# Weight loads in two halves, a limit on the bytes in flight, and a new order of the first 840 pieces of a pooled-attention and gated-MLP kernel

## The chip, the cores and the metric

The kernel runs on one core of a Trainium2 chip. The metric is the device time of one execution in microseconds (us). Engines are named as the profile names them: PE is TensorE (matmuls), PEld its weight loads, DVE is VectorE, ACT is ScalarE, POOL is GpSimd, and SP is the queue that issues the DMA transfers.

## The reference

For each of 8 batches and 8 heads (576 positions, 64 wide) two attentions are added: one over queries, keys and values averaged in groups of 4 (144 positions), repeated 4 times, and a banded one in which position i sees the positions less than 4 away. The heads joined give x, 576 x 512 per batch. An MLP with a spatial gate follows.

```python
def _attn_ref(q, k, v):
    q_d = q.reshape(B, H, Sd, factor, D).mean(axis=3)
    out_up = np.repeat(sm_attn(q_d, k_d, v_d), factor, axis=2)
    mask = np.abs(pos[:, None] - pos[None, :]) < factor
    scores = np.where(mask, scale * np.matmul(q, k.transpose(0, 1, 3, 2)), -1000000000.0)
    ...
    return (out_up + np.matmul(attn, v)).astype(np.float32)

def _moe_ref(x, w_in, g_ln, w_sg, b_sg, w_out):
    h = x @ w_in
    h = 0.5 * h * (1.0 + np.tanh(c * (h + 0.044715 * h ** 3)))
    u, v = (h[..., :d_ff // 2], h[..., d_ff // 2:])
    v_n = (v - mu) / np.sqrt(var + 1e-06) * g_ln
    v_s = np.einsum('ts,bsd->btd', w_sg, v_n) + b_sg[None, :, None]
    return (x + (u * v_s) @ w_out).astype(np.float32)
```

`w_in` is 512 x 1024, `w_sg` 576 x 576, `w_out` 512 x 512.

## The kernel before

The work is cut into 2,109 named pieces. Each piece is a small function that emits the instructions of one step, and `ORDER` is a stored list of the names, in which they are emitted. A letter behind a slash says which engine does a piece that several could do (V is VectorE, A ScalarE, P GpSimd). All engines take their instructions in this order, so `ORDER` sets each engine's queue, the SP queue among them. `place` hands out the numbered buffers (8 of PSUM, 10 called X, 38 called R) along the same list.

The 64 heads are taken as 32 pairs g = 0 to 31, four per batch. The pieces of a pair: `lq`, `lk`, `lv`, `lw` load query, key, the values for the averaged attention and the values for the band; `qs`, `ks` sum groups of 4; `S` and `Y` are the band's and the averaged scores (`YS` both together from pair 4 on); `mx`/`my` take row maxima, `ia`/`ib` subtract them from the first pairs' scores, `ea`/`eb`/`es`/`ec` are exponentials and their sums, `re`/`rc` reciprocals, `np`/`nq` normalise; `T`, `t`, `U` transpose the probabilities on TensorE, `pa` to `pe` copy them to SBUF; `D` is the product with the values; `oe`, `od`, `xa`, `xb` merge the two attentions into x; `xh`, `xl`, `xc` split x in a high and a low part, since the dense matmuls run in a rounded format and are done three times (high x high, high x low, low x high).

The weights arrive as 64-bit words. `w_in`'s second half comes as `wy0` to `wy3`, its first half as `wz0` to `wz3`, `w_out` as `wr0` to `wr3`, each 512 KB; `wq0` to `wq4` are `w_sg`'s rows. For each of the first twelve, `w` loads it, `wu` scales the low word (ScalarE), `wq` scales the high word (VectorE or ScalarE), `wb` moves its bits (two VectorE instructions), `wt` adds (GpSimd), and `wh`, `wl` make the high and the low part. Of the MLP of batch b, `vk`, `v` are the gate's matmuls (of batch 0 one per pair, line 743), `u` those of the other half, `s` the spatial matmul, `o` the last one (line 821); the rest is activation, normalisation and stores.

Transfers are issued by `dma` on the SP queue. A transfer waits until the one issued six before it has landed (`DEPTH = 6`). `S0` and `S3` are preceded by 28 and 20 matmuls on zeros (line 976).

Of the kernel before, what the change touches and what calls it, by code (L numbers as in the profile page):

```python
# [94 lines left out]
wuy3 wqy3/A nq2/P U2 t2 xa0 xb0 ks5/P wby1 xh0/A YS4 pb2/A pc2/A nq3/P np3/P xl0/P t3 lw1 wuy1 wty1 pe2/A whz0/A
wlz0/P ma4 my4 ny4/A mb4 U3 wz2 wqz2/A lv2 ec4 T3 pa3/A pb3/V pc3/A pe3/A D1 mx4 wby3 wty3 lq5 qs5/V wbz2 nx4/A why1/A
wly1/P oe1/A od1 lw3 wuz2 YS5 ma5 vk3.0 xa1 xb1 vk1.0 lv3 ea4 mb5 vk0.0 wtz2 mx5 eb4 whz2/A re4/A my5 ny5/V lw2 nx5/A
D2 why3/A xh1/V ec5 vk2.0 wty2 xl1/V vk3.1 lv4 vs4 D3 wlz2/V rc4 nq4/P wr2 why2/A wly2/P oe2/V od2 xa2 xb2 wq0 wz1 lq6
eb5 ea5 xh2/A wq1 np4/V vk2.1 oe3/V od3 xa3 vk0.1 xb3 xh3/V xl3/P whq0/A U4 xl2/V wly3/V whq1/A wqz1/A t4 re5/A T4
pa4/A vk1.1 pb4/A pc4/A wur2 wbz1 wuz1 xc2 xc0 xc1 vk0.2 wtz1 wqr2/V wbr2 rc5 nq5/P lv5 lk6 np5/P ks6/V pe4/A vk2.2  # L100
v0.2 vg0.2 wq2 wq3 whq3/A wlq3/P vk1.2 v0.0 vg0.0 qs6/V vb0.2 v0.1 vg0.1 lw4 D4 YS6 whq2/A whz1/A wlz1/P my6 ny6/A lq8
ma6 mb6 ec6 mx6 nx6/A oe4/V wlq1/V lk7 vs5 wlq0/P vk3.2 od4 xa4 T5 vk4.0 eb6 vk4.1 ks7/V pa5/V vb0.0 vp0.0 lq7 qs7/V
vk4.2 ea6 re6/A u0.4 rc6 qs8/V u0.2 xb4 t5 u0.5 ua0.4 xc3 v0.4 ua0.5 ua0.2 U5 va0.4/A pb5/V pc5/A vb0.1 u0.3 nq6/P
np6/P lk8 v0.3 ks8/V pe5/A lw5 D5 lv6 ua0.3 vp0.2 vg0.3 vn0.0 vh0.0/A lw7 wr1 wr3 YS7 lw6 vp0.1 vn0.1 wq4 whq4/A b lq9
wlq2/V vj0.4 ma7 vl0.0/P mb7 vh0.1/A vs6 vl0.1/P T6 vg0.4 vn0.2 oe5/V pa6/A my7 ny7/V ec7 wlq4/P u0.7 vb0.3 vb0.4
vp0.3 od5 xa5 t6 u0.6 ua0.6 u0.1 ua0.7 vp0.4 U6 pb6/A mx7 pc6/A pe6/V vh0.2/A u0.0 xb5 xh5/A ua0.0 vn0.4 vn0.3 vh0.4/V
vh0.3/V vl0.3/P ua0.1 nx7/A ea7 eb7 re7/A vl0.2/V D6 YS8 lk10 vl0.4/V s0.0 s0.2 my8 wr0 wqr3/V ma8 oe6/V mb8 mx8 lv7
sa0.0 od6 vs7 lk9 sm0.0/V xa6 xb6 ny8/A s0.3 s0.1 rc7 lq10 ec8 xh4/A s0.4 wbr3 sa0.2 np7/V T7 pa7/A nq7/V ks9/V U7
ks10/V nx8/A qs10/V wur0 pb7/A pc7/A sa0.1 t7 pe7/A s0.5 wqr1/A wur3 sm0.2/P sa0.4 D7 xh6/A xl5/P wqr0/V qs9/V YS9 lv8
lk11 lq11 sm0.4/V eb8 sm0.1/P sa0.3 sm0.3/P xl6/P wbr1 s0.6 ma9 oe7/V od7 xa7 xb7 ea8 xl4/P re8/A s0.7 mb9 mx9 nx9/V  # L110
wur1 sa0.5 wtr3 xh7/A xl7/P v1.2 rc8 my9 sm0.5/V eb9 ny9/A ec9 np8/V T8 nq8/V u1.1 ea9 pa8/V t8 re9/A wbr0 gh0.2/A
sa0.7 wtr1 whr1/V whr3/A sa0.6 vg1.2 vb1.2 rc9 lw8 U8 pb8/A pc8/A pe8/A gh0.1/A np9/V v1.1 vg1.1 xc7 vs8 D8 oe8/A od8
xa8 lv9 YS10 ks11/V ma10 mb10 xb8 u1.4 qs11/V mx10 nx10/V u1.0 ua1.0 ua1.1 wtr0 v1.0 vp1.2 vs9 nq9/P wlr3/V my10 vb1.1
wlr1/P vp1.1 gl0.2/V xc6 whr0/V T9 ea10 pa9/A U9 pb9/V ny10/V xh8/V wlr0/V gl0.1/V gh0.0/A lk12 ec10 ks12/V pc9/V t9
pe9/V sm0.6/V u1.3 xl8/V u1.2 ua1.2 wtr2 xc5 whr2/A ua1.4 wlr2/V u1.5 xc4 u1.6 lq12 vn1.1 ua1.3 lw9 vg1.0 vb1.0 D9
ua1.5 YS11 ma11 mb11 eb10 re10/A sm0.7/P gl0.0/P my11 v1.3 v1.4 vp1.0 vn1.0 gh0.3/V gl0.3/V o0.2 vg1.3 rc10 np10/P T10
nq10/V oe9/V od9 xc8 lv10 vs10 ua1.6 lq13 va1.4/A o0.4 vh1.1/A vj1.4 vg1.4 ny11/A ec11 vb1.4 vp1.4 lw10 pa10/V xa9
o0.0 vn1.2 vn1.4 vh1.2/V xb9 o0.6 t10 qs12/P u1.7 oa0.2 vh1.0/A U10 mx11 vh1.4/A oa0.0 pb10/A vb1.3 pc10/V pe10/V
oa0.4 vl1.4/V oa0.6 vl1.2/P vp1.3 nx11/A eb11 o0.3 ea11 vn1.3 oa0.3 vl1.0/V o0.7 oa0.7 re11/A rc11 D10 YS12 my12
ny12/A lv11 oe10/V vl1.1/P vh1.3/A vl1.3/P qs13/V np11/P ma12 mb12 o0.1 oa0.1 lk14 lw11 od10 nq11/P mx12 s1.0 sa1.0  # L120
o0.5 xa10 T11 xb10 U11 pa11/V ec12 sm1.0/V ks14/P nx12/A eb12 s1.2 sa1.2 pb11/V ea12 re12/A rc12 xh10/A xl10/V s1.4
t11 oa0.5 pc11/A pe11/A nq12/V s1.1 sa1.1 sm1.2/V sa1.4 vs11 D11 oe11/A od11 lk13 os0.0 xh9/A ks13/P YS13 lk15 my13
np12/P ma13 mb13 xa11 xb11 ny13/A xl9/V s1.3 xh11/A t12 sm1.4/V U12 sm1.1/P sa1.3 s1.6 mx13 nx13/A T12 pa12/A pb12/V
pc12/A pe12/A s1.5 s1.7 xl11/P sm1.3/P gh1.1/A sa1.5 sm1.5/V lq14 ec13 os0.2 lv12 os0.3 v2.0 u2.6 ks15/P eb13 vs12
qs14/P sa1.6 ea13 re13/V ua2.6 rc13 ua1.7 vg2.0 v2.3 os0.1 np13/P T13 pa13/A gh1.0/V gl1.0/P lw12 sm1.6/V D12 lv13
oe12/A sa1.7 sm1.7/V gh1.3/V gl1.3/V gl1.1/V YS14 nq13/P U13 od12 xa12 gh1.2/A lw13 t13 vg2.3 vb2.0 xc11 ma14 mb14
gl1.2/P lq15 o1.4 my14 pb13/V xb12 ny14/V vs13 mx14 v2.1 ec14 lq16 o1.0 pc13/V nx14/A vp2.0 vn2.0 vh2.0/V pe13/V D13
oa1.4 ea14 qs15/V eb14 oa1.0 YS15 my15 re14/V ny15/V ec15 ma15 mb15 mx15 rc14 v2.2 vg2.2 lk16 xc10 xc9 v2.4 lv14 vg2.1
vs14 np14/V vb2.1 T14 lw14 va2.4/A vj2.4 nx15/A nq14/P vl2.0/V oe13/A od13 xa13 xb13 ks16/P vp2.1 qs16/V vn2.1 vh2.1/A
# [906 lines left out]
```

## Time and profile before

| what | us |
|---|---|
| median of 3 runs | 577.85 (575.29 to 580.2) |
| the profiled execution | 577.51 |
| span in it, first to last instruction | 575.7 |
| mean granted TensorE clock | 0.993 |

The profile cuts the span into stretches and says how long each engine was busy in each. A row of the order of time gives start, length, engine, line, operation, what is written and read, a count, and in brackets how long the engine idled before and what released it ("issue" is time for which the profile shows no releaser). The span is read against TensorE: what its matmuls take is fixed by the computation, so its idle time is what an order can change.

### The profile page before, as it was taken

How to read it: one execution, taken by the hardware profiler on the slowest of the kernel's cores; microseconds unless marked ns; L12 is line 12 of the kernel's file. 1: busy time of each engine (PE TensorE's matmuls, PEld its weight loads, DVE VectorE, ACT ScalarE, POOL GpSimd, SP SyncE). 2: the span in 40 equal slices, each digit the busy share in tenths (PEclk: the TensorE clock that was granted, in tenths of full speed). 3: DMA queues.
4: the chain of work that ended last, by engine and by line, in shares of the span. 5: the costliest groups of instructions: out<-in, count | busy, mean ns of one | idle time of the engine just before them, and what ended most of it. 6: DMA issues, size and time to landing. Idle time of an engine off the chain costs nothing.

```text
span 575.7 us, 17465 instructions
## 1 busy us (share of the span) xinstructions
PE 557.2 (97%) x7032; PEld 521.3 (91%) x7032; DVE 422.9 (73%) x944; ACT 343.9 (60%) x1165; POOL 314.7 (55%) x395
## 2 busy tenths in 40 slices
...
GB/s 291 281 251 332 164 148 84 41 60 77 121 158 173 23 109 55 210 59 2 87 56 201 134 44 99 53 139 98 104 66 196 105 106 2 17 23 41 43 1 102
DMA packets 30608, 62.73 MB, mean 109 GB/s; under 512 B 3648, under 2 KB 3904, under 8 KB 30528
## 3 DMA queue, kind: packets, MB, share of 16 engines
...
## 4 chain that ended last, share of the span: by engine, by line
PE 77%; DVE 3%; ACT 2%; DMA 0%; issue 0%; ACTq 0%
PE ps L821 50%; PE ps L743 14%; PE ps L558 2%; PE ps L619 2%; PE ps L635 2%; PE ps L567 2%; PE ps L456 2%; PE ps L477 2%; ACT L538 1%; ACT pd L538 1%; DMA R<-in_v_dram 0%; DVE X L552 0%; DVE X L464 0%; DVE R L642 0%; DVE kd L423 0%
## 5 line engine op out<-in xcount | busy, mean ns | idle before, releaser
L821 PE MATMUL ps<-wsg_h,R 128*128 128x288 f32 x576 | 121.3, 298 | 1.0 <-DVE R L342 1.0
L821 PE MATMUL ps<-X,weight_z 128*128 128x288 f32 x512 | 109.9, 298 | 0.0
L821 PE MATMUL ps<-R,weight_r 128*128 128x288 f32 x768 | 108.5, 297 | 1.0 <-ACT R L755 0.7
L821 PEld LDWEIGHTS ps<-R,weight_r 128*128 128x128 f32 x768 | 103.5, 188 | 2.0 <-ACT R L755 0.9
L743 PE MATMUL ps<-weight_y,X 128*128 128x512 f32 x320 | 97.5, 398 | 0.0
L821 PEld LDWEIGHTS ps<-wsg_h,R 128*128 128x128 f32 x576 | 94.0, 188 | 1.4 <-DVE R L342 1.1
L516 ACT ACTIVATE X<-X,nb 128x64 f32<-128x64 f32 x280 | 93.6, 340 | 2.3 <-DVE nb L495 1.8
L821 PE MATMUL ps<-wsg_l,R 128*128 128x288 f32 x320 | 92.5, 295 | 0.0
L821 PEld LDWEIGHTS ps<-X,weight_z 128*128 128x128 f32 x512 | 84.4, 188 | 0.4
L821 PE MATMUL ps<-R,weight_z 128*128 128x288 f32 x256 | 75.5, 295 | 0.0
L859 DVE SCALAR_TENSOR_TENSOR vs<-ps,g_sb,b_sb 128x288 f32<-128x288 f32 x64 | 32.7, 514 | 52.4 <-PE ps L821 48.5
L743 PEld LDWEIGHTS ps<-weight_y,X 128*128 128x128 f32 x320 | 58.1, 188 | 12.0 <-DVE weight_y L357 0.3
L784 POOL TENSOR_TENSOR rs<-rs,nhalf 128x1 f32<-128x1 f32 (+1 forms) x40 | 23.9, 599 | 68.5 <-DVE rs L775 66.7
L232 ACT CAST R<-R 128x512 fp32r<-128x512 f32 (+2 forms) x40 | 25.4, 643 | 59.5 <-DVE R L866 32.1
L821 PEld LDWEIGHTS ps<-wsg_l,R 128*128 128x128 f32 x320 | 60.3, 188 | 0.0
L516 ACT ACTIVATION_READ_ACCUMULATOR X<-X,nb 128x1 f32 x280 | 53.6, 192 | 0.0
L812 POOL TENSOR_TENSOR R<-R,R 128x512 fp32r<-128x512 f32 (+1 forms) x24 | 32.6, 1362 | 33.9 <-ACT R L232 7.7
L743 PE MATMUL ps<-weight_y,R 128*128 128x512 f32 x128 | 50.4, 394 | 0.0
L440 POOL TENSOR_TENSOR pairs<-R 112x256 f32<-112x256 f32 x56 | 45.2, 808 | 9.4 <-DMA R<-in_v_dram 9.4
L866 POOL TENSOR_TENSOR R<-R,vs 128x288 f32<-128x288 f32 x27 | 24.9, 922 | 44.6 <-DVE vs L859 30.4
L821 PEld LDWEIGHTS ps<-R,weight_z 128*128 128x128 f32 x256 | 48.2, 188 | 0.2
L232 ACT COPY R<-ps 112x288 f32<-112x288 f32 (+4 forms) x83 | 31.0, 410 | 28.3 <-PE ps L558 18.0
...
## 6 DMA issues: line engine op xcount, KB each, us to landing
...
R<-in_kT_dram SPq DMA_DIRECT2D x32, 293.0 KB, 4.2
R<-in_qT_dram SPq DMA_DIRECT2D x32, 293.0 KB, 3.9
...
weight_z<-in_w_in_dram SPq DMA_DIRECT2D x4, 512.0 KB, 5.8
weight_y<-in_w_in_dram SPq DMA_DIRECT2D x4, 512.0 KB, 5.9
weight_r<-in_w_out_dram SPq DMA_DIRECT2D x4, 512.0 KB, 5.6
```

Of the source, the lines that this page charges most:

```text
L232: (nc.scalar.copy if e == "A" else ENG[e].tensor_copy)(**kw)
L440: ENG[e].tensor_tensor(out=pairs, in0=v[:, 0:2], in1=v[:, 2:4], op=ALU.add)
L456: nc.tensor.matmul(out=sp[i][os, c * KB:(c + 1) * KB], lhsT=q[hs, t * QB:t * QB + KB], rhs=k[hs, t * QB:t * QB + KB], start=not early, sto ...
L477: nc.tensor.matmul(out=st["sdv"][n][os, cs], lhsT=qd2[par][hs, i * QC:i * QC + HD], rhs=st["kd"][hs, ks], start=True, stop=True)
L516: nc.scalar.activation(out=st["ms"][:, t, :], in_=src, func=AF.Exp, bias=st["nb"][:, t:t + 1], scale=scale, accum_out=sums[par][:, t:t + 1])
L538: nc.scalar.activation(out=pd[:, n], in_=st["sdv"][n].rearrange("p (c k) -> p c k", c=3), func=AF.Exp, bias=st["nbd"][:, n:n + 1], scale=s ...
L743: nc.tensor.matmul(out=acc, lhsT=r32(l), rhs=r32(weights[f"y{k}"][:, 0, w]), start=(i == 0 and ks[0] == 0), stop=(i == len(ops) - 1 and ks ...
L784: nc.gpsimd.tensor_tensor(out=rs[0:n], in0=rs[0:n], in1=nhalf[0:n], op=ALU.pow)
L812: ENG[e].tensor_tensor(out=r32(dst), in0=vact[s][0][0:n], in1=vh[0:n, 0:DM], op=ALU.subtract)
L821: nc.tensor.matmul(out=acc[:, 0:HALF], lhsT=r32(l), rhs=r32(r), start=(first and n == 0), stop=(last and n == len(ops) - 1))
L859: nc.vector.scalar_tensor_tensor(out=vsb[i], in0=at["ps", "m", b, "s", i][:, 0:HALF], scalar=g_sb[:, i // 2:i // 2 + 1], in1=b_sb[:, half( ...
L866: ENG[e].tensor_tensor(out=u[:, half(i)], in0=u[:, half(i)], in1=vsb[i], op=ALU.mult)
```

## The change

Three things change. Each of the twelve 512 KB weight loads becomes two of 64 rows, one after the other. The limit of six transfers becomes a limit in bytes: a transfer waits for the newest earlier one with which it and all issued since would exceed 1,250 KB, or for the ninth back. And the stored order differs in its first 840 pieces (none is added or removed); 108 pieces change their engine over it: 33 from VectorE to ScalarE, 26 from ScalarE to VectorE, 26 from VectorE to GpSimd, 23 from GpSimd to VectorE. No arithmetic changes.

```diff
-wz3 wuz3 lk0 ks0/P wqz3/V wbz3 wy0 wqy0/V wby0 lq0 lk2 lk1 wtz3 whz3/A wlz3/P S0 lq1 qs0/V Y0 mx0 ia0 lq3 my0 ks1/P
+wy0 wqy0/A wuy0 wby0 lq0 lk0 ks0/V S0 mx0 ia0 ib0 qs0/P lk2 Y0 my0 lk1 wty0 lq1 S1 ks1/P lq2 S2 mx1 ea0 qs1/P Y1 ny0/A
...
-DEPTH = 6
+DEPTH, FLYING = 9, 1250 * 1024
...
     def dma(e, **kw):
-        move = DQ[e].dma_start(**kw)
-        if len(moves) >= DEPTH:
-            tc.add_manual_dep(move.ins, moves[-DEPTH].ins.name, mybir.DependencyInfo(mybir.DependencyClass.Sync, mybir.DependencyReason.DATA))
-        moves.append(move)
+        move, size = DQ[e].dma_start(**kw), 4 * math.prod(kw["out"].shape)
+        ahead, flying = 0, size
+        while ahead < len(moves) and ahead < DEPTH and flying <= FLYING:
+            ahead += 1
+            flying += moves[-ahead][1]
+        if flying > FLYING or ahead == DEPTH:
+            tc.add_manual_dep(move.ins, moves[-ahead][0].ins.name, mybir.DependencyInfo(mybir.DependencyClass.Sync, mybir.DependencyReason.DATA))
+        moves.append((move, size))
...
         def load(e):
             weights[t] = buffers.tile(shape, F32, name=f"weight_{t}")
-            dma("S", out=flat().bitcast(I32), in_=src)
+            for rows in (slice(0, HALFP), slice(HALFP, P)):
+                dma(e, out=flat().bitcast(I32)[rows], in_=src[rows])
```

The SP queue at the start of the program, before (R are keys and queries; the names DMAHW are the landings waited for):

```order
L224 DMA weight_z_149<-in_w_in_dram 128x2x512
L224 DMA R_152<-in_kT_dram 128x586
L224 DMA weight_y_162<-in_w_in_dram 128x1024
L224 DMA R_169<-in_qT_dram 128x586
L224 DMA R_171<-in_kT_dram 128x586
L224 DMA R_173<-in_kT_dram 128x586
L224 DMA R_232<-in_qT_dram 128x586 [waits DMAHW0_49]
```

The same place after:

```order
L226 DMA weight_y_149<-in_w_in_dram 64x1024 x2
L226 DMA R_158<-in_qT_dram 128x586
L226 DMA R_160<-in_kT_dram 128x586
L226 DMA R_224<-in_kT_dram 128x586 [waits DMAHW0_49]
L226 DMA R_238<-in_kT_dram 128x586 [waits DMAHW1_49]
L226 DMA R_241<-in_qT_dram 128x586 [waits DMAHW2_49]
```

weight_z's first load has moved behind the first four pairs' queries and keys, and the fifth transfer already waits for a landing, where before it was the seventh.

VectorE behind its set-up, before (weight_z and weight_y are pieces of the weights, qd the query's sums, stats the maxima, X the centred scores of pair 0):

```order
L336 TENSOR_SCALAR weight_z_149<-weight_z_149 128x512
L292 MEMSET mask_sb 128x3
L293 MEMSET mask_sb 128x7
L340 TENSOR_SCALAR ps_158<-weight_z_149 128x512
L342 SCALAR_TENSOR_TENSOR R_159<-weight_z_149,ps_158 128x512
L336 TENSOR_SCALAR weight_y_162<-weight_y_162 128x512
L340 TENSOR_SCALAR ps_165<-weight_y_162 128x512
L342 SCALAR_TENSOR_TENSOR R_166<-weight_y_162,ps_165 128x512
L423 TENSOR_REDUCE qd_80<-R_169 128x144
L486 TENSOR_REDUCE stats_84<-ps_208 128x4
L486 TENSOR_REDUCE stats_84<-ps_209 128x6
L525 TENSOR_TENSOR X_247<-ps_208,stats_84 128x256
```

The same place after:

```order
L298 MEMSET mask_sb 128x3
L299 MEMSET mask_sb 128x7
L347 TENSOR_SCALAR ps_154<-weight_y_149 128x512
L349 SCALAR_TENSOR_TENSOR R_155<-weight_y_149,ps_154 128x512
L430 TENSOR_REDUCE kd_88<-R_160 128x144
L493 TENSOR_REDUCE stats_84<-ps_192 128x4
L493 TENSOR_REDUCE stats_84<-ps_193 128x6
L532 TENSOR_TENSOR X_218<-ps_192,stats_84 128x256
L532 TENSOR_TENSOR X_218<-ps_193,stats_84 128x384
```

The three weight_z instructions and the scaling of weight_y no longer stand ahead of pair 0; the sum of the key has come to VectorE and the query's has gone.

ScalarE at the start, before:

```order
L346 ACT_TABLE_LOAD
L346 ACTIVATE weight_z_149<-weight_z_149 128x512
L232 CAST weight_z_176<-R_159 128x2x256
L346 ACTIVATE weight_y_162<-weight_y_162 128x512
L529 ACTIVATE X_247<-X_247 128x640
```

The same place after:

```order
L341 ACT_TABLE_LOAD
L341 ACTIVATE weight_y_149<-weight_y_149 128x512
L353 ACTIVATE weight_y_149<-weight_y_149 128x512
L536 ACTIVATE X_218<-X_218 128x640
```

Both scalings of weight_y are ScalarE's now, and nothing of weight_z is ahead of pair 0's exponential.

More of the change, by code (lines that the diff above doesn't have):

```diff
@@ L1 @@
+import math
 from contextlib import ExitStack
@@ L32 @@
 HALF = S // 2
+HALFP = P // 2
 NS = 5
@@ L95 @@
[L95 to L129, printed above, removed]
@@ new lines @@
+ec0 qs2/P lq3 qs3/P wy1 es0 re0/A ia1 rc0 np0/P why0/A lk3 S3 lw0 my1 ny1/A nq0/P U0 ks2/P ib1 mx2 ec1 ia2 ks3/P ib2
+ea1 wuy1 ea2 es1 mx3 ia3 wly0/P T0 es2 ib3 re1/A rc1 np1/P nq1/P pa0/A pb0/A Y2 pc0/A t0 wqy1/A Y3 wy3 wqy3/A wuy3
+pe0/A lv0 D0 U1 ea3 my2 ny2/A ec2 my3 ny3/A wby1 wty1 es3 oe0/V re2/A rc2 np2/P od0 xa0 xb0 wy2 lk4 wuy2 wqy2/A T1
+pa1/A pb1/A lq4 nq2/P qs4/P wby2 pc1/A t1 ks4/V pe1/A ec3 re3/A rc3 nq3/P np3/P why1/A xh0/A lv1 lw1 D1 oe1/A wz3 wuz3
+wqz3/A xl0/P lv2 YS4 wby3 my4 ma4 mb4 ny4/A T2 pa2/A od1 U2 pb2/V pc2/A xa1 xb1 t2 pe2/V U3 ec4 T3 pa3/A mx4 pb3/V
@@ new lines @@
+pc3/A wbz3 wz2 wqz2/A wbz2 wq1 whq1/A wuz2 nx4/A wty3 why3/A ea4 t3 pe3/A lw2 D2 lq5 vk3.0 wlq1/V lk5 ks5/V oe2/A
+vk1.0 od2 lv3 wty2 wly1/P xc0 qs5/P YS5 xa2 xb2 eb4 xh1/A my5 ny5/A wtz3 ma5 mb5 why2/A mx5 wq2 lw3 D3 vk0.0 xl1/V
+vk0.1 vk3.1 re4/A wly3/P wtz2 xh2/A vk1.1 xl2/V xc2 wz1 wqz1/V vk2.0 vk2.1 wly2/V vk3.2 ec5 lv4 whz2/A rc4 np4/P T4
+wlz2/V wbz1 nq4/P oe3/A od3 xa3 xb3 lk6 ks6/V nx5/A wz0 lw4 wuz1 wtz1 lq6 ea5 U4 vk0.2 t4 wq3 vk1.2 eb5 re5/A rc5
+small xc1 xh3/A lq7 xl3/V np5/V nq5/V wqz0/A wbz0 wuz0 xc3 v0.0 vk2.2 vg0.0 v0.1 v0.3 vs4 pa4/A pb4/V whq2/A vb0.0
@@ new lines @@
+xh10/A T11 xh9/A nq11/P s1.0 sa1.1 sa1.0 s1.7 sm1.0/V pa11/A lv11 mx12 nx12/V ny12/A sm1.1/P ec12 U11 t11 pb11/V
+pc11/A pe11/V xc8 lq13 qs13/V vs11 s1.2 sa1.2 oa0.7 D11 lv12 xl10/P YS13 lk15 oe11/V od11 s1.5 gh1.0/A ks15/V ea12
+xl9/P ma13 eb12 re12/A rc12 mb13 mx13 my13 xa11 xb11 xh11/A nx13/A s1.3 s1.4 nq12/P np12/P sa1.3 t12 sm1.3/V T12
+sm1.2/P sa1.4 gh1.1/A ea13 xl11/V v2.0 sm1.4/V pa12/V eb13 sa1.5 os0.3 sm1.5/P ny13/V lq14 s1.6 qs14/V ec13 vg2.0
+re13/V xc11 os0.0 U12 sa1.6 lw13 u2.6 pb12/V sa1.7 pc12/A pe12/A lq15 vs12 D12 YS14 lv13 lk16 lq16 rc13 vb2.0 nq13/V
```

156 lines of the change are left out of this document (88 added, 68 removed).

## The prediction

> **What bounds the kernel now.** I read the head of the page first, then busy time by stretch, then TensorE's instructions in order of time with the idle time before them. First the head of the page and the stretches (stretch: length, busy time of each engine with its instructions, granted clock, share of the DMA engines, GB/s):
>
> ```profile
> span 575.7 us, 17465 instructions
> PE 557.2 (97%) x7032; PEld 521.3 (91%) x7032; DVE 422.9 (73%) x944; ACT 343.9 (60%) x1165; POOL 314.7 (55%) x395
> ...
> 0.00:8.50 8.50, 5.29 (x31) 3.64 (x31) 5.30 (x26) 1.99 (x2) 3.98 (x13) 1.00 0.74 246
> 8.50:25.00 16.50, 13.15 (x265) 10.52 (x267) 15.55 (x35) 10.67 (x36) 13.86 (x18) 0.89 0.99 313
> 25.00:38.50 13.50, 11.68 (x352) 10.88 (x347) 12.20 (x27) 12.93 (x45) 13.05 (x14) 0.88 0.78 242
> 38.50:51.00 12.50, 9.43 (x230) 7.75 (x225) 9.43 (x19) 11.33 (x54) 8.56 (x9) 1.00 0.99 311
> 51.00:65.00 14.00, 13.27 (x170) 10.98 (x169) 13.52 (x27) 10.07 (x25) 10.24 (x11) 1.00 0.98 326
> 80.00:110.00 30.00, 28.56 (x397) 26.99 (x396) 29.37 (x57) 25.08 (x103) 20.63 (x22) 1.00 0.24 75
> 110.00:575.70 465.70, 460.86 (x5399) 436.17 (x5397) 324.01 (x725) 258.53 (x866) 231.16 (x296) 1.00 0.28 86
> ```
>
> TensorE is the bound: 557.2 of 575.7 us. It is idle for 18.5 us, and 12.2 of these lie before 65 us (65 less 5.29, 13.15, 11.68, 9.43 and 13.27). From 110 us on it idles 4.8 us in 465.7, and there the change alters little. So what can be won or lost lies in the first 65 us, where all is scarce at once: from 8.5 to 38.5 us VectorE, GpSimd and, from 25 us, ScalarE are busy above 80% and mostly above 90%, and the DMA engines run at 0.98 or 0.99 in three of the four stretches after 8.5. These are TensorE's rows at which it waits, or which I use as marks (start, length, what, count, idle before and its releaser):
>
> ```profile
> 8.50 0.93 PE L456 MATMUL ps<-R,R 64*64 64x64 f32 x40 [2.05 <-DMA R<-in_qT_dram]
> 11.03 1.11 PE L477 MATMUL ps<-kd,qd 64*64 64x144 f32 x16 [1.60 <-DVE qd L423]
> ...
> 23.27 0.40 PE L567 MATMUL ps<-turn_p,pd 112*112 112x112 f32 x2 [1.69 <-POOL pd L555]
> ...
> 25.05 0.50 PE L619 MATMUL ps<-R,R 48*64 48x144 f32 x1
> ...
> 33.41 0.31 PE L567 MATMUL ps<-turn_p,pd 112*112 112x112 f32 x1 [1.39 <-issue]
> ...
> 38.55 0.74 PE L743 MATMUL ps<-weight_y,X 128*128 128x512 f32 x2
> ...
> 40.84 1.71 PE L619 MATMUL ps<-R,R 48*64 48x144 f32 x60
> ...
> 43.73 0.68 PE L635 MATMUL ps<-R,X 64*64 64x58 f32 x30 [0.91 <-issue]
> ...
> 45.94 1.71 PE L619 MATMUL ps<-R,R 48*64 48x144 f32 x60
> ...
> 50.31 0.45 PE L635 MATMUL ps<-R,X 64*64 64x58 f32 x13 [2.16 <-issue]
> ...
> 60.22 0.53 PE L477 MATMUL ps<-kd,qd 64*64 64x144 f32 x11 [0.73 <-DVE qd L423]
> ```
>
> The reader is to see three kinds of loss: the first scores (S0) wait for q until 8.50; three holes of 1.39, 0.91 and 2.16 us (4.46 in all) have no releaser in the profile; and the first output product, D0, starts only at 25.05, the fourth, D3, at 45.94. The nine dense matmuls between 38.55 and 40.84 cost 0.25 us each.
>
> **The change part by part.** First what feeds S0: single transfers, KB, and us from issue to landing, then a lone key load issued at 73.6 us.
>
> ```profile
> 0.74 0.44 SPq L224 DMA_DIRECT2D weight_z<-in_w_in_dram  x1
> 1.23 0.46 SPq L224 DMA_DIRECT2D R<-in_kT_dram  x1
> 1.74 0.42 SPq L224 DMA_DIRECT2D weight_y<-in_w_in_dram  x1
> 2.20 0.43 SPq L224 DMA_DIRECT2D R<-in_qT_dram  x1
> ...
> weight_z<-in_w_in_dram SPq DMA_DIRECT2D x1, 512.0 KB, 4.4
> ...
> R<-in_kT_dram SPq DMA_DIRECT2D x1, 293.0 KB, 4.6
> ...
> R<-in_qT_dram SPq DMA_DIRECT2D x1, 293.0 KB, 6.2
> ...
> R<-in_kT_dram SPq DMA_DIRECT2D x1, 293.0 KB, 3.0
> ```
>
> The first 512 KB land at 0.74 + 4.4 = 5.1 us, the key at 5.8, the query at 8.4. So 805 KB (weight_y and the query) take 2.6 us, 317 GB/s. After the change only weight_y (512 KB), query and key stand ahead of S0: 600 KB (in decimal) behind the first landing, 1.9 us at that rate, 1.5 us at 400. S0 starts at about 6.8 instead of 8.50: 1.7 us.
>
> From S0 to D0. The instructions needed, on VectorE, ScalarE and GpSimd:
>
> ```profile
> 7.56 1.21 DVE L336 TENSOR_SCALAR weight_y<-weight_y 128x512 f32<-128x512 f32 x1 [0.49 <-DMA weight_y<-in_w_in_dram]
> 8.80 0.69 DVE L340 TENSOR_SCALAR ps<-weight_y 128x512 int32<-128x512 int32 x1
> 9.53 0.69 DVE L342 SCALAR_TENSOR_TENSOR R<-weight_y,ps 128x512 int32<-128x512 int32 x1
> 10.14 0.75 DVE L423 TENSOR_REDUCE qd<-R 128x144 f32<-128x576 f32 x1
> 10.80 0.88 DVE L486 TENSOR_REDUCE stats<-ps 128x4 f32<-128x256 f32 x2
> 11.60 0.41 DVE L525 TENSOR_TENSOR X<-ps,stats 128x256 f32<-128x256 f32 x1
> ...
> 12.77 0.55 DVE L525 TENSOR_TENSOR X<-ps,stats 128x384 f32<-128x384 f32 x1
> ...
> 13.35 0.74 ACT L529 ACTIVATE X<-X 128x640 f32<-128x640 f32 x1 [3.64 <-DVE X L525]
> ...
> 17.87 1.26 POOL L552 TENSOR_TENSOR X<-X,rc 128x640 f32<-128x640 f32 x1 [1.38 <-DVE rc L549]
> ```
>
> Before, VectorE works through weight_z's and weight_y's pieces before it touches pair 0, and pair 0's centred scores are done at 13.3. After, it has weight_y alone, and its scaling moves to ScalarE (5.15 to 5.85). Start to start the two bit steps take 0.72 + 0.61 (till 7.2), the key's sum 0.66 (7.9), the maxima 0.80 (8.7), the two subtractions 0.33 + 0.47 (9.5). So pair 0 is 3.8 us earlier. Behind it, ScalarE's copies gate D0: counted from the changed program's rows with the durations of this trace, ScalarE has 10.9 us of work up to the last copy that D0 reads; it starts late by 3.9 us (first landing), waits 3.1 for pair 0's scores, and I allow 1.6 for shorter waits: D0 at 19.5, against 25.05. That is 5.55 us, of which 1.7 are S0's. But 12 transposes that stood ahead of D0 now stand behind it, 1.0 us by their pace in this trace. Net 4.5. Bounds: 2 us, if the order only passes on S0's 1.7 and the clock stays as it was; 6, if the 1.6 us of waits vanish.
>
> From D0 to D3. It took 20.9 us. TensorE's own work in it is 17.4 us before and 16.3 after (rows by pace). ScalarE now has 14.6 us of work between the copies that D0 and D3 wait for, against 9.2: the scaling of the weights that was VectorE's. At the 96% that it reached from 25 to 38.5 us this takes 15.2, so it does not exceed TensorE's. GpSimd and VectorE hold transposes and YS4, YS5 back for some 2 us more. I take 18.5, and 2.5 for holes without a releaser, as before 2.3 (1.39 and 0.91) fell in this part: 21.0, so D3 at 40.5. Bounds 18.8 (TensorE's work and the holes alone) and 23. Ahead of D3 stood 15 dense matmuls, and now stand 6: nine of 0.25, 2.2 us, are still to be done. Net at D3: 45.9 less 40.5 less 2.2, 3.2 us ahead.
>
> After D3, the kernel before loses the hole of 2.16 and 0.73 us at a wait for a query sum; I take half of it for the changed one: 1.5 us gained (0 to 2.9). From 80 to 110 us VectorE is busy 29.37 of 30 us, so a lead must be paid for by its own lead; the moved pieces leave VectorE some 5 us less work in the whole (rows by duration), so I take back only 0.3.
>
> Priced at nothing: twelve more issues of 0.48 us (0.74, 1.23, 1.74: start to start) make 5.8 us on the SP queue over some 100 us; it mostly waits for landings there; uncovered, each delays the next input by 0.48. The limit of 1,250 KB keeps four of the 293 KB loads in flight; a lone one lands after 3.0 us, so 1.2 MB per 3.0 us, 400 GB/s, is allowed, and 242 to 326 were moved. Only at the start does it bite: the fifth load leaves at the first landing and lands near 7.5 to 8, up to 1.3 us after the fourth; the second pair needs it at about 9. Two more loads of the function table (54 against 52) fall on ScalarE, which has 4.9 of 30 us free between 80 and 110.
>
> [...]
>
> The sum: 3.2 + 1.5 - 0.3 = 4.4 us. The profiled execution took 577.51 us, 0.34 under the median of 577.85; 577.5 less 4.4 is 573.1, so 573.0, 0.8% under the median.
>
> **The rivals.**
> 1. The lead is given back. VectorE has 0.63 us free between 80 and 110 us, and the lead there needs VectorE to have waited less before. For it: in no other place is another engine so full. Against it: before 65 us VectorE idled 9 us (65 less 5.30, 15.55, 12.20, 9.43 and 13.52). If two thirds go back, 576.0.
> 2. More than I take. The granted clock was 0.89 and 0.88 from 8.5 to 38.5 us, 1.8 + 1.6 us lost. If the denser start keeps it at 1.00, and the holes shrink to half because fewer bytes are queued, a further 3.4 + 2.0 come on top, less what ScalarE then holds up: 568.5. [...]
> 3. Slower: the inputs come late. D3's last input stands after 10.2 MB in the new queue. At 310 GB/s it lands at 5.1 + 9.7/0.310 = 36.4, 4 us before its use. Under 274 GB/s it is late, and under 211 GB/s the kernel is over 1% slower: at 200 it lands at 53.6, 13 us late, and the time is 586. For it: four in flight instead of six, and 64-row parts. Against it: the 400 GB/s above, and 313 with 48-row parts in the queue (8.5 to 25 us).
>
> **How the numbers follow.** My forecast has 0.50 (570 to 575.5), rival 1 0.23, rival 2 0.18, rival 3 0.09. A measurement of this kernel can tell about 1% from no change (the three runs shown lie 575.29 to 580.2). Faster by over 1%, under 572.1, are rival 2 and some four tenths of the first case: 0.18 + 0.19 = 0.37. Slower by over 1%, over 583.6, is most of rival 3: 0.07. The rest, 0.56, lies within 1%. The range, from rival 2's time less 0.5 to rival 1's with 2 us on it, is 568 to 578; it leaves out rival 3 and the edge of rival 2.
>
> **What would show it.** S0 at 6.5 to 7.2 us; pair 0's subtractions done before 10; D0 at 18 to 21.5 and D3 at 38 to 43; ScalarE above 90% between D0 and D3; DMA still near 300 GB/s up to 50 us; TensorE idle some 8 us before 65 instead of 12.2. It is wrong if D3 waits for an input (a DMA named as releaser), if a hole without a releaser grows over 2.5 us, or if TensorE waits for VectorE between 80 and 110 by more than 2 us.

## The result, and the profile after

The changed kernel takes 580.3 us (median of 11 runs, 578.25 to 583.96), the kernel before, beside it, 576.74 (11 runs, 574.51 to 580.2): a ratio of 1.0061, with a 95% interval of 1.0033 to 1.0089. So it is 0.6% slower, where 0.8% faster was forecast, and it lies outside the forecast's range. The profiled execution took 582.08 us; its span is 580.3. One run of the experiments below, 586.89 us of the kernel without the limit in bytes, was in a slow state and is left out of its ratio.

The busy time by stretch of the changed kernel (columns as in the prediction):

```profile
0.00:8.50 8.50, 5.96 (x70) 4.32 (x70) 3.21 (x23) 2.53 (x3) 2.70 (x12) 1.00 0.69 212
8.50:25.00 16.50, 13.92 (x323) 11.12 (x323) 15.10 (x35) 11.15 (x38) 13.86 (x19) 0.90 0.87 231
25.00:38.50 13.50, 8.75 (x232) 7.78 (x225) 10.48 (x24) 8.71 (x29) 11.18 (x12) 0.99 0.81 224
38.50:51.00 12.50, 10.93 (x254) 9.45 (x249) 7.87 (x15) 10.46 (x43) 5.06 (x6) 0.74 0.84 230
51.00:65.00 14.00, 14.00 (x173) 11.54 (x172) 13.09 (x30) 12.98 (x40) 11.42 (x14) 1.00 0.86 256
...
80.00:110.00 30.00, 28.55 (x343) 26.79 (x343) 25.51 (x55) 27.78 (x90) 21.48 (x26) 1.00 0.57 160
```

The last two columns carry the result. From 8.5 to 51 us the DMA engines now move 231, 224 and 230 GB/s, where they moved 313, 242 and 311. That is 9.7 MB instead of 12.3 (GB/s times length), and the missing 2.6 MB are over 8 us of transfers. From 25 us on the other engines have slack: ScalarE is busy for 8.71 of 13.5 us, VectorE then for 7.87 of 12.5. So no computing engine has become the bound; the inputs come late. TensorE's rows at which it waits, and its marks:

```profile
7.62 0.93 PE L463 MATMUL ps<-R,R 64*64 64x64 f32 x40 [1.38 <-DMA R<-in_kT_dram]
...
10.12 0.77 PE L484 MATMUL ps<-kd,qd 64*64 64x144 f32 x16 [1.56 <-DVE kd L430]
...
21.44 0.46 PE L626 MATMUL ps<-R,R 48*64 48x144 f32 x4
...
22.86 1.61 PE L626 MATMUL ps<-R,R 48*64 48x144 f32 x54 [0.96 <-DMA R<-in_v_dram]
...
28.43 2.02 PE L626 MATMUL ps<-R,R 48*64 48x144 f32 x62 [1.98 <-DVE R L349]
...
36.63 0.64 PE L565 MATMUL ps<-turn_l,X 122*128 122x122 f32 x4 [2.75 <-ACT R L238]
...
45.78 1.94 PE L626 MATMUL ps<-R,R 48*64 48x144 f32 x64
...
47.52 0.79 PE L642 MATMUL ps<-R,X 64*64 64x58 f32 x34
...
49.87 0.33 PE L642 MATMUL ps<-R,X 64*64 64x58 f32 x6 [1.57 <-issue]
```

S0 starts at 7.62 and D0 at 21.44, both ahead of the kernel before (8.50 and 25.05). But D3 starts at 45.78, where it stood at 45.94, and nine dense matmuls that were done by then are still to come. A DMA is named only in two of the waits. The two longest name ScalarE and VectorE, which are far from full (8.71 and 10.48 of 13.5 us in that stretch). ScalarE, which lets the transposes at 36.63 go, had itself waited for a weight until just before:

```profile
34.82 0.68 ACT L353 ACTIVATE weight_z<-weight_z 128x512 int32<-128x512 uint32 x1 [3.46 <-DMA weight_z<-in_w_in_dram]
```

For the wait at 28.43 the profile does not settle it: VectorE's instruction ends at 28.3, and so does the first load of values that this product reads (issued at 23.80, 4.5 us to landing). The last input of D3, the values of its band, comes late too; the row of its issue, and from the DMA view its size and the us to landing:

```profile
43.70 0.35 SPq L226 DMA_DIRECT2D X<-in_vw_dram  x1
```

```profile
X<-in_vw_dram SPq DMA_DIRECT2D x1, 320.0 KB, 3.8
```

It lands at 43.70 + 3.8 = 47.5, and the product that reads it starts at 47.52. But TensorE does not idle before that product: it is busy without a break from 36.63 to 48.3 us, so what put D3 back lies ahead of 36.63, and in the low clock behind it (0.71 in that stretch). The issue at 43.70 shows the limit at work: a key load issued at 38.10 took 5.5 us to land, to 43.6, and from 42.5 to 43.5 us, while it and the loads behind it still counted, the DMA engines were busy for 0.12 and then 0.06 of the time.

### The profile page after: what moved, and what is told of

It is laid out like the page before. It is cut to its first block, busy times and chain, and to the rows that moved or that the text cites. A ratio compares the mean times of both kernels' runs of the same rounds, so it can differ in the third digit from the quotient of the medians.

```text
span 580.3 us, 17514 instructions
## 1 busy us (share of the span) xinstructions
PE 560.3 (97%) x7032; PEld 523.0 (90%) x7032; DVE 413.5 (71%) x934; ACT 350.5 (60%) x1174; POOL 314.1 (54%) x397
## 4 chain that ended last, share of the span: by engine, by line
PE 81%; DMA 10%; ACT 4%; DVE 3%; issue 1%; SPq 1%; POOL 1%; ACTq 0%; POOLq 0%
PE ps L828 52%; PE ps L750 15%; DMA R<-in_qT_dram 3%; PE ps L626 2%; PE ps L565 2%; PE ps L642 2%; PE ps L484 2%; PE ps L463 2%; PE ps L574 2%; DMA weight_z<-in_w_in_dram 2%; DMA weight_y<-in_w_in_dram 2%; DMA R<-in_w_sgT_dram 1%; DMA R<-in_v_dram 1%; SPq L226 1%; DMA R<-in_kT_dram 1%
## 5 line engine op out<-in xcount | busy, mean ns | idle before, releaser
L750 PE MATMUL ps<-weight_y,X 128*128 128x512 f32 x320 | 98.7, 402 | 0.0
L238 ACT CAST R<-R 128x512 fp32r<-128x512 f32 (+2 forms) x43 | 27.2, 643 | 60.6 <-DVE R L873 32.1
L238 ACT COPY R<-ps 128x464 f32<-128x464 f32 (+4 forms) x78 | 29.7, 413 | 21.4 <-PE ps L565 11.2
```

The source lines that it names most:

```text
L238: (nc.scalar.copy if e == "A" else ENG[e].tensor_copy)(**kw)
L750: nc.tensor.matmul(out=acc, lhsT=r32(l), rhs=r32(weights[f"y{k}"][:, 0, w]), start=(i == 0 and ks[0] == 0), stop=(i == len(ops) - 1 and ks ...
```

## The experiments

The change has three parts: the order, the limit of 1,250 KB, and the parts of 64 rows. The first four kernels take them apart. Each is timed in three rounds beside the same runs of the kernel before (577.44 us, 31 runs); the changed kernel's own row in the table is the measurement above, beside 576.74.

**The changed kernel without the parts of 64 rows.** Edit of the changed kernel:

```diff
-            for rows in (slice(0, HALFP), slice(HALFP, P)):
-                dma(e, out=flat().bitcast(I32)[rows], in_=src[rows])
+            dma("S", out=flat().bitcast(I32), in_=src)
```

> The changed kernel with whole 128-row weight loads, its limit of 1,250 KB and its order kept. Three theories: (H) the 64-row halves move slowly and hold up all that is queued with them; (C) the byte limit leaves the DMA engines without work whenever one transfer is slow; (O) the new order needs more than any transfers can give. H expects the DMA rate from 8.5 to 51 us back from about 230 to 290 GB/s or more, D0 at 20 us or earlier instead of 21.5 to 22.9, and 573 to 576 us. C expects no more than 240 GB/s and 579 to 583 us, and as a whole 512 KB load takes more of the 1,250 KB, rather worse than the change. O expects 580 us with the rate changed or not.

**The changed kernel without the limit in bytes:**

```diff
-DEPTH, FLYING = 9, 1250 * 1024
+DEPTH = 6
...
-        move, size = DQ[e].dma_start(**kw), 4 * math.prod(kw["out"].shape)
...
+        move = DQ[e].dma_start(**kw)
+        if len(moves) >= DEPTH:
```

> The changed kernel with the old limit of six transfers, its halves and its order kept. C expects the rate back above 280 GB/s and 573 to 576 us. H expects about 230 GB/s still and 578 to 581 us (six transfers of 256 to 300 KB are 1.7 MB, so the queue is deeper by a third). O expects 580 us.

**The new order alone** (both edits together):

> Only the new order: whole loads and the limit of six transfers, as before the change. H and C both expect 571 to 575 us, faster than before (my forecast was 573), with D0 near 19.5 us. O expects 578 us or more with the DMA rate near 300 GB/s.

**The old order with the limit in bytes and the parts of 64 rows** (the changed kernel with the `ORDER` of before):

> The old order with the new transfers (halves and the byte limit). H and C expect it slower than before, 580 to 585 us, with the DMA rate from 8.5 to 51 us near 230 GB/s. O expects it within 1 us of before, 577 us.

| kernel | order | limit | weights | us | ratio to before (95%) |
|---|---|---|---|---|---|
| order alone | new | six | whole | 574.38 | 0.9943 (0.9918 to 0.9969) |
| without the parts | new | 1,250 KB | whole | 580.17 | 1.0053 (1.0026 to 1.0079) |
| without the limit in bytes | new | six | 64 rows | 579.55 | 1.0021 (0.9987 to 1.0054) |
| changed kernel | new | 1,250 KB | 64 rows | 580.3 | 1.0061 (1.0033 to 1.0089) |
| old order, both | old | 1,250 KB | 64 rows | 581.36 | 1.0062 (1.0032 to 1.0091) |

The order alone gains 0.57%, 574.38 us, close to the 573.0 forecast for the whole change. Either part of the transfers alone takes it away, and the two together cost little more than the limit alone. The theory that the order is bad falls. How the transfers take the gain away shows in the stretches. The order alone, from 8.5 to 51 us:

```profile
8.50:25.00 16.50, 14.73 (x348) 12.01 (x352) 15.87 (x38) 14.47 (x50) 15.70 (x21) 0.98 0.89 296
25.00:38.50 13.50, 11.95 (x333) 10.65 (x329) 11.65 (x25) 11.42 (x43) 13.12 (x13) 0.90 0.89 268
38.50:51.00 12.50, 8.79 (x122) 7.31 (x117) 9.63 (x20) 10.11 (x43) 4.79 (x7) 0.86 0.99 313
```

The new order with the limit in bytes, whole loads:

```profile
8.50:25.00 16.50, 13.26 (x319) 10.77 (x318) 13.89 (x35) 11.63 (x39) 13.81 (x19) 1.00 0.76 237
25.00:38.50 13.50, 10.55 (x243) 9.89 (x244) 9.02 (x20) 9.49 (x31) 10.00 (x11) 0.75 0.68 212
38.50:51.00 12.50, 7.59 (x217) 6.38 (x211) 10.29 (x21) 9.98 (x42) 6.57 (x7) 0.95 0.76 233
```

The new order with parts of 64 rows and the limit of six:

```profile
8.50:25.00 16.50, 14.12 (x339) 11.34 (x334) 16.04 (x39) 12.21 (x41) 14.53 (x20) 1.00 0.94 257
25.00:38.50 13.50, 12.19 (x287) 11.55 (x288) 10.51 (x23) 10.28 (x33) 10.49 (x11) 0.75 0.83 245
38.50:51.00 12.50, 8.14 (x172) 6.69 (x171) 9.89 (x19) 10.52 (x51) 7.06 (x8) 0.83 0.90 215
```

The reader should divide the last column by the one ahead of it: GB/s by busy share is the pace at which the engines move while they are busy. For the order alone it is 333, 301 and 316. With the limit in bytes it is much the same, 312, 312 and 307, but the share has fallen from 0.89, 0.89, 0.99 to 0.76, 0.68, 0.76: the engines run dry. With parts of 64 rows the share is nearly kept, 0.94, 0.83, 0.90, but the pace has fallen to 273, 295 and 239: the engines are busy and slow. These are two mechanisms. The changed kernel has some of each: shares of 0.87, 0.81, 0.84, paces of 266, 277, 274. The gaps can be seen in the DMA view of 8.5 to 51 us, busy tenths in 40 slices, first of the order alone, then with the limit in bytes:

```profile
DMA  9999996879987489999989968789999999998999
```

```profile
DMA  9797974978228897448999306997998457899656
```

**How the slow transfers become time.** Only in part as idle time of TensorE. What its matmuls take is not fixed by the computation alone, as was said above of the kernel before. Its busy time in the profiled execution is 557.2 us before and 560.3 in the changed kernel, its idle time 18.5 and 20.0. The granted clock has a share in this: in these traces it falls to 0.50 or 0.51, before from 11.2 to 14.6 and from 24.9 to 28.3 us, in the changed kernel from 10.8 to 14.2 and from 38.1 to 45.0. In that last stretch three dense matmuls of 128 x 512 take 1.41 us (43.15 to 44.56, start to start), at the full clock 0.69 (50.94 to 51.63). The time lost to it can be estimated for every run, not only the profiled one, as span times one less the mean granted clock; it is the most that the clock can have cost, if TensorE's work goes in proportion to it as these three do, since time in which TensorE idles anyway is counted too. Means over the runs (the spans are some 1.8 us shorter than the times):

| kernel | span, us | lost to the clock, us |
|---|---|---|
| before | 575.5 | 3.4 |
| order alone | 572.8 | 2.4 |
| without the parts (limit in bytes) | 578.7 | 6.1 |
| without the limit in bytes (parts) | 577.3 | 5.3 |
| changed kernel | 578.8 | 5.3 |

So of the 5.9 us that the limit costs in the new order up to 3.7 go through the clock, and of the 4.5 that the parts cost up to 2.9. Among all the kernels timed here, each with 1,250 KB, with four transfers or with parts of 64 rows loses 5.3 us or more to the clock, and each other one 4.1 or less. The edits touch the transfers alone, so the lower clock follows from them; what makes it fall was not tested.

**The old order with one part each**, the same two edits made to the kernel before (577.23 us beside them, 25 runs):

> The old order and whole 128-row weight loads, with the limit of 1,250 KB alone. Theory F (too few bytes in flight leave the DMA engines idle between transfers): from 8.5 to 51 us the engines' busy share falls from the 0.99, 0.78, 0.99 of the kernel before to about 0.75, while the GB/s divided by the share stay near 312; time 579 to 582, ratio 1.004 to 1.009. Rival R (the limit hurts only together with the new order, which asks for the inputs sooner): ratio within 0.998 to 1.002.

> The old order and the limit of six transfers, with the weights in parts of 64 rows alone. Theory H (64-row parts move slower): the busy share stays near 0.95 and the GB/s divided by the share fall from 316 to about 270, while the parts are in the queue; time 578 to 580, ratio 1.001 to 1.006. Rival R (the old order has slack for it): ratio within 0.998 to 1.001 with the same lower rate.

The limit in bytes: 580.81 us, ratio 1.0054 (1.0024 to 1.0085). The parts of 64 rows: 582.23, ratio 1.0081 (1.0044 to 1.0119), more than I had expected of them. Their stretches, of the first and then of the second:

```profile
8.50:25.00 16.50, 13.76 (x258) 10.81 (x262) 15.37 (x35) 9.82 (x35) 13.72 (x17) 0.79 0.82 266
25.00:38.50 13.50, 10.77 (x279) 9.25 (x283) 10.52 (x23) 9.71 (x31) 10.79 (x12) 0.87 0.74 229
```

```profile
8.50:25.00 16.50, 12.09 (x244) 9.41 (x244) 13.56 (x32) 8.61 (x25) 13.44 (x19) 0.79 0.85 247
25.00:38.50 13.50, 9.28 (x208) 7.28 (x211) 11.32 (x26) 10.15 (x36) 10.74 (x12) 1.00 0.90 240
```

The paces are 324 and 309 with the limit, 291 and 267 with the parts: the same two signatures, though the share of the second is lower than the 0.95 expected. The old order has no slack for either. In it the limit in bytes costs 3.6 us, in the new order 5.8 (580.17 less 574.38), which would fit that the new order needs its inputs earlier; the intervals (0.3% each way) leave open whether the two differ.

**Loads alone.** A kernel without any computation, which leaves only transfers in its trace:

```diff
+STAGES = (("whole", 6), ("whole", 2), ("rows64", 6), ("rows64", 4), ("columns", 6), ("columns", 4), ("low64", 6), ("keys", 6), ("keys", 4), ("keys", 3))
...
+        for kind, deep in STAGES:
+            first = True
+            for i in range(20 if kind == "keys" else 12):
+                for kw in locals()[kind](i):
+                    dma(1 if first else deep, **kw)
+                    first = False
```

> No computation: the kernel only loads, in ten stages that each start with an empty queue, and stores zeros; its output is zeros. Stages of 6 MB: whole weights (128 rows of 4 KB) with 6 and with 2 outstanding; parts of 64 rows with 6 and with 4; parts of 512 columns (128 rows of 2 KB) with 6 and with 4; lower halves of 64 rows only with 6; then 293 KB keys with 6, 4 and 3. Theory F: whole weights fall from 310 or more GB/s with 6 (3 MB in flight) to 240 or less with 2 (1 MB); the keys from 300 or more with 6 to about 240 with 4 and 200 with 3, the engines' share falling with them. Theory H: the parts of 64 rows move at 270 or less with 6 outstanding though the share is near 1, the lower halves alone no faster than 250, and the parts of 512 columns at 300 or more. Rival N (number and size of the transfers cost, not their rows): the parts of 512 columns are as slow as the parts of 64 rows. Rival C (the loads are slowed by other traffic of the full kernel): every stage is near 310 GB/s.

Its stages, each from its first to its last packet (length, VectorE, GpSimd, clock, share, GB/s); in order whole weights with 6 and with 2 outstanding, 64 rows in turn lower and upper with 6, 512 columns with 6, lower halves only with 6, and keys with 6, 4 and 3:

```profile
1.75:19.77 18.02, 0.00 (x0) 0.00 (x0) 1.00 0.92 349
21.19:49.56 28.37, 0.00 (x0) 0.00 (x0) 1.00 0.69 222
51.20:78.16 26.96, 0.00 (x0) 0.00 (x0) 1.00 0.99 233
109.22:130.95 21.73, 0.00 (x0) 0.00 (x0) 1.00 0.88 290
158.00:188.89 30.89, 0.00 (x0) 0.00 (x0) 1.00 0.99 204
190.61:207.27 16.66, 0.00 (x0) 0.00 (x0) 1.00 0.99 360
208.68:229.07 20.39, 0.00 (x0) 0.00 (x0) 1.00 0.91 294
230.40:249.50 19.10, 0.00 (x0) 0.00 (x0) 1.00 0.87 273
```

Two whole weights outstanding, all that 1,250 KB allows, move 222 GB/s instead of 349; four keys 294 instead of 360 (I had expected the keys to fall further, to 240). The pace falls a little as well, from 379 to 322 with the whole weights, so the share does not hold all of it. No other traffic is needed for it, so the rival that blamed the rest of the kernel falls (the last row, keys with 3, holds the first stores besides). Parts of 64 rows move 233 GB/s at a share of 0.99, and the lower halves alone 204. Parts of 512 columns, of the same size and number, move 290, a little under the 300 expected, so it is not size or number that makes the 64 rows slow. With four outstanding instead of six the parts of 64 rows still move 227, against 233: with these slow packets the shorter queue cost little. This fits that the two costs do not add up in the changed kernel.

**The same question in the kernel, and other limits**, all in the new order, three rounds (before: 577.23 us beside the first, 577.77 beside the rest):

```diff
-DEPTH = 6
+DEPTH = 8
```

> The new order with whole loads and a limit of eight transfers in place of six. Theory F: more in flight cannot lose bandwidth; the share is 0.9 or more from 8.5 us on and the time is that of the order alone, 574.4, or up to 2 us less; ratio 0.990 to 0.996. Rival Q (with more queued, each input that is needed soon lands later): 575 to 578, ratio 0.996 to 1.001.

```diff
-            dma("S", out=flat().bitcast(I32), in_=src)
+            n, m = src.shape[1:]
+            for part in (slice(0, 1), slice(1, 2)) if n == 2 else (slice(0, m // 2), slice(m // 2, m)):
+                cut = (slice(None), part) if n == 2 else (slice(None), slice(None), part)
+                dma(e, out=flat().bitcast(I32)[cut], in_=src[cut])
```

> The new order and the limit of six transfers; each weight load in two parts of 512 columns (all 128 rows, 2 KB of a row) instead of two parts of 64 rows. Theory H (it is the 64 rows that are slow): the median packet keeps its duration, GB/s divided by share is near 310 from 8.5 to 51 us, and the time is that of the order alone or a little more, since six parts are fewer bytes: 574 to 576.5, ratio 0.993 to 0.998. Rival N (the number and size of the transfers cost): as with 64-row parts, 578 to 580, ratio 1.000 to 1.004.

```diff
-DEPTH = 6
+DEPTH = 4
```

> The new order, whole loads, a limit of four transfers: 1.2 MB of the 293 KB loads as under the limit of the change, but up to 2 MB of the weights, where the change allows 1 MB. Theory F: the loads of keys alone moved 277 GB/s with four and the weights 212 with two, so this stands between the order alone and the order with the limit: share 0.80 to 0.88 from 8.5 to 51 us, 575.5 to 579, ratio 0.996 to 1.002. Rival W (only the weights' two at a time cost anything): 574 to 575, ratio 0.992 to 0.996.

```diff
-DEPTH, FLYING = 9, 1250 * 1024
+DEPTH, FLYING = 9, 1800 * 1024
```

> The new order, whole loads, the change's limit in bytes raised to 1,800 KB (three weights, six keys). Theory F: bandwidth comes back with the bytes: share 0.85 to 0.95, 574.5 to 577, ratio 0.994 to 0.999. Rival S (what costs is that a limit in bytes makes a load wait for the newest earlier one that it must, not how many bytes fly): 579 to 581, as with 1,250 KB.

The new order alone once more, in five rounds:

> The new order alone again, with more rounds, beside the other three on one chip: 573 to 576, ratio 0.990 to 0.997, under the kernel before and under the changed one. If it lies above 0.999, the gain of the order alone was chance.

| new order with | us | ratio (95%) | share, 8.5 / 25 / 38.5 us on | pace, GB/s |
|---|---|---|---|---|
| four transfers | 579.04 | 1.0029 (0.9998 to 1.0061) | 0.77 / 0.75 / 0.74 | 327 / 327 / 308 |
| 1,800 KB | 573.79 | 0.9926 (0.9892 to 0.9959) | 0.92 / 0.92 / 0.94 | 327 / 300 / 307 |
| six, again | 575.57 | 0.9944 (0.9917 to 0.9970) | 0.87 / 0.90 / 0.96 | 343 / 303 / 313 |
| eight | 576.32 | 0.9970 (0.9942 to 0.9998) | 0.99 / 0.97 / 1.03 | 325 / 309 / 310 |
| six, parts of 512 columns | 576.34 | 0.9971 (0.9940 to 1.0002) | 0.85 / 0.85 / 0.96 | 324 / 296 / 310 |

The limit's size is the cause, not its form: 1,800 KB gives the whole gain, 1,250 KB none, and four transfers, which I expected between, cost nearly as much as the limit in bytes (just outside my 0.996 to 1.002, on the side of theory F). So it is not only the weights' two at a time. Eight outstanding fill the engines but gain no more: 0.9970 lies where rival Q had it, not theory F, though the intervals leave open whether they lose something against six. Parts of columns keep the pace of whole loads, as the theory has it; their time against the parts of 64 rows (0.9971 against 1.0021) is not separated by the intervals. Six parts of either kind also hold fewer bytes than six whole loads, so some of what the parts cost may be that. The gain of the order came again. The 1,800 KB version, better than its 0.994 to 0.999, and the order alone both beat the kernel before and the changed one, and can't be told from each other.

**Why 64 rows are slow.** Loads alone once more, with other sets of rows:

```diff
+    def rows64(i):
+        yield part(i, slice(0, HALFP))
+        yield part(i, slice(HALFP, P))
...
+    def evens64(i):
+        yield part(i, slice(0, P, 2))
+        yield part((i + 6) % 12, slice(0, P, 2))
...
+    def quarter32(i):
+        for k in range(4):
+            yield part((i + 3 * k) % 12, slice(0, 32))
```

> No computation, zeros stored: ten stages of loads as before. Whole weights with 6, 4 and 3 outstanding; then, with 6 outstanding, 64-row parts in turn lower and upper; the upper halves only; 64 rows spread over all partitions (every second one), in turn even and odd; the even ones only; 32-row parts in turn; the lowest 32 rows only; last 293 KB keys with 8 outstanding. Theory P (the range of partitions that is written sets the pace): every second row moves at a packet time near 159 ns and 260 GB/s or more, though it is 64 rows as well; the upper halves only are as slow as the lower were (204 GB/s); the lowest 32 rows only go at 120 or less. Rival K (the count of rows in a transfer, so four for each engine instead of eight): every second row is as slow as the halves, 230, with packets near 275 ns. Theory F for the whole weights: 349 GB/s with 6, about 310 with 4, about 270 with 3, against 222 with 2; keys with 8 no faster than the 360 with 6.

Its stages: whole weights with 4 and with 3 outstanding; then with 6 the halves in turn, the upper halves only, every second row in turn even and odd, the even rows only, 32 rows in turn, and the lowest 32 rows only:

```profile
20.70:39.60 18.90, 0.00 (x0) 0.00 (x0) 1.00 0.91 333
40.90:62.30 21.40, 0.00 (x0) 0.00 (x0) 1.00 0.87 294
64.00:91.30 27.30, 0.00 (x0) 0.00 (x0) 1.00 1.00 231
93.40:124.10 30.70, 0.00 (x0) 0.00 (x0) 1.00 1.01 205
126.20:148.00 21.80, 0.00 (x0) 0.00 (x0) 1.00 0.85 288
149.70:170.40 20.70, 0.00 (x0) 0.00 (x0) 1.00 0.88 303
171.70:198.90 27.20, 0.00 (x0) 0.00 (x0) 1.00 0.97 231
200.50:231.30 30.80, 0.00 (x0) 0.00 (x0) 1.00 1.01 204
```

And the median duration of a 4 KB packet in these stages, and in the full kernels from 12 to 25 us, from the packets of the traces:

```
loads alone: whole 159 ns; halves in turn 284; upper only 320; every second row 159; lowest 32 rows 324
full kernels: before 159 ns; order alone 159; with 1,250 KB 159; with parts of 64 rows 259; changed 211
```

64 rows spread over all partitions go at the packet time of whole loads (159 ns, against 284 to 324 for neighbouring rows), so the count of rows is not it: what counted in these stages is which partitions were written. The lowest 32 rows move 204 GB/s, as the lowest 64 did; here my number (120 or less) was wrong, and for whole weights with 4 and with 3 the 310 and 270 were too low (333 and 294). The halves in turn moved 231 to 233, 13% more than one half alone (204 and 205). Why neighbouring rows are slower no run shows.

## Why the prediction failed, point by point

- **S0 at 6.8.** It came at 7.62, since the first inputs were slower (212 GB/s to 8.5 us; 264 in the order alone). In the order alone S0 starts at 6.57: the step holds there.
- **Pair 0 done before 10, D0 at 19.5, D3 at 40.5.** In the changed kernel pair 0's subtractions end at 11.6, D0 starts at 21.44, D3 at 45.78. In the order alone they end at 9.2, and its marks are, as TensorE's rows have it:

```profile
6.57 0.93 PE L458 MATMUL ps<-R,R 64*64 64x64 f32 x40 [0.40 <-DMA R<-in_kT_dram]
...
18.14 0.33 PE L621 MATMUL ps<-R,R 48*64 48x144 f32 x1
...
38.08 1.85 PE L621 MATMUL ps<-R,R 48*64 48x144 f32 x58
...
44.35 0.33 PE L637 MATMUL ps<-R,X 64*64 64x58 f32 x6 [3.71 <-issue]
```

  D0 at 18.14 and D3 at 38.08 are 1.4 and 2.4 us ahead of the forecast and inside the bounds given, so for the order the working held in the main. Not in all: from D0 to D3 ScalarE was to be above 90%; it is at 89% (17.75 of 19.94 us), and GpSimd is the fullest, at 98% (19.55). That the order alone ends at 574.38, so near to 573.0, is partly luck: what it had gained on the forecast at D3 went into the hole of 3.71 us.
- **The limit, priced at nothing: the step that failed.** "A lone one lands after 3.0 us, so 1.2 MB per 3.0 us, 400 GB/s, is allowed." The landing time of a lone load was put in for that of a load among others. The keys took 5.4 us to land between 8 and 40 us in the changed kernel (row of its DMA view, KB and median us):

```profile
R<-in_kT_dram SPq DMA_DIRECT2D x3, 293.0 KB, 5.4
```

  So 1.2 MB in 5.4 us are 222 GB/s, against 231 and 224 measured. With the limit but whole loads the keys took 5.1 us, which gives 235, against 237 and 212. Even with nothing but keys on the queue four move 294, which is 1.2 MB in 4.1 us and not in 3.0. And four loads of 293 KB are the most that the limit lets fly; of the 512 KB weights it is two, which by themselves move 222.
- **The halves, priced at twelve issues of 0.48 us.** The price was their pace instead: loads alone moved 233 GB/s in halves in turn, 349 whole. Rival 3 names the 64-row parts with no number for what they cost, and I weighed them with the 313 GB/s of the stretch with 48-row parts, which holds 0.8 MB of those in 5.2 MB.
- **After D3, 1.5 us gained from the hole of 2.16 and the wait of 0.73.** In the changed kernel the hole is 1.57 and the wait is gone, so 1.3 us are gained: right there. In the order alone the hole is 3.71 and 0.8 us are lost. The term was a guess, with no working of what sets the hole.
- **Rival 1, the lead given back.** Not at 80 to 110 us, where TensorE idles 1.45 us, and 0.18 in the order alone. But some of it goes later: in the order alone ScalarE holds up a product at 158 us for 1.15 us. The start of TensorE's 5,400th and 1,000th matmul from the end, in us:

```
             5,400th   1,000th   end of span
before        109.7     457.6     575.7
order alone   106.5     455.5     573.8
changed       113.2     462.3     580.3
```

  Of the order's 3.2 us of lead at the first mark 2.1 are left at the second. The changed kernel is 3.5 behind at the first, 4.7 at the second.
- **Rival 2, more than I took.** The clock did not stay at 1.00: 0.90 and 0.86 in two stretches of the order alone, 0.74 from 38.5 to 51 us in the changed kernel, which costs up to 12.5 x 0.26 = 3.2 us there. By the same sum over the stretches from 8.5 to 51 us the changed kernel loses 5.0 us, the kernel before and the order alone 3.4 each. The rival had the clock as something to win; it was also something to lose. That a denser start holds it up was a guess of mine, which was not tested. The holes without a releaser did shrink before 65 us, from 4.46 us to 1.57, but that the fewer bytes queued are the cause is not shown.
- **The signs named.** No DMA is named as releaser at D3, so that sign did not come as it was put. It came ahead of D3: TensorE waits 0.96 us for D0's values, and 2.75 us for ScalarE, which had waited for a weight. ScalarE, to be above 90% between D0 and D3, is at 78% (18.92 of 24.34 us), and DMA at 224 to 231 GB/s, to be near 300. No hole without a releaser is over 2.5 us in the changed kernel. TensorE idles 11.4 us before 65 us, against 12.2 before the change and 8.9 in the order alone; 8 were forecast. So the idle time alone would have called the changed kernel the faster one up to there.
- **Rival 3, the inputs come late (0.09).** This is what came. Its own working with the pace measured: 9.7 MB at 230 GB/s land the last input of D3 at 5.1 + 42.2 = 47.3 (measured 47.5), 6.8 us behind the forecast D3 of 40.5, so 573.0 + 6.8 = 579.8, against 580.3. The pace and the landing it had right. That the time comes out so near is partly luck: TensorE reached that product at 47.5 without a wait for it, and the low clock, through which some of the time went, is not in the working. Its chance was too small, because the 400 GB/s spoke against it.

## What to carry to other kernels

In the changed kernel the rate followed the bytes in flight divided by the landing time of a load in the full queue (1.2 MB in 5.4 us are 222 GB/s, and 231 and 224 were measured), not of a lone one (3.0 us, 400 GB/s). So work a limit out with the former: here 1,250 KB were too few and 1,800 KB were enough (310 GB/s for 5.4 us are 1.7 MB). Price a split of a load along the partitions by the partitions that each part writes: here 64 neighbouring rows, lower and upper in turn, moved 231 to 233 GB/s, two thirds of the 349 of whole loads; 512 columns of all rows or every second row moved 288 to 303. Read the share of the DMA engines beside the GB/s: here a fallen share (0.68 to 0.76, at a pace of 307 to 312) was a dry queue, a full share with few GB/s (0.99 at 233) was slow packets (284 ns against 159), and each had another cure: 1,800 KB in flight the first, whole loads or parts of 512 columns the second. Read TensorE's busy time and its granted clock beside its idle time: here 3.1 of the 4.6 us by which the changed kernel's profiled span is longer are busy time.

## What the runs showed besides

TensorE's holes of 0.88 us and more without a releaser, 14 in the traces of the 13 kernels that compute, end 2.3 to 2.7 us after a 16 KB transfer on the queue that the page of the profile calls instruction (q8) has started. Eight of them, from the packets of the traces:

```
                          start of the transfer   TensorE goes on   after   idle
before                         30.80                  33.41          2.61    1.39
before                         41.26                  43.73          2.47    0.91
before                         47.60                  50.31          2.71    2.16
changed                        47.27                  49.87          2.60    1.57
order, 1,250 KB, whole         47.20                  49.70          2.50    2.34
order alone                    41.69                  44.35          2.66    3.71
order, eight                   41.31                  43.73          2.42    4.54
order, four                    43.28                  45.58          2.30    1.00
```

That TensorE waits there for its own code is a guess from the queue's name, which no run tests. The time after the start is much the same with a short queue of data as with a long one (2.30 us with four transfers, 2.42 with eight, 2.50 with 1,250 KB), so in these runs a limit on the data in flight did not make such a transfer quicker once it had started. What sets its start was not tried; the hole is longest, 4.54 us with eight transfers and with 1,800 KB, where TensorE reaches the place earliest, at 39.2 and 39.4 us.
